# An adaLN block on one core: the second token pair's transposes and splits move up to two steps ahead, the down weights' combinations one step, the odd tile's weights to the end, and one more side of weights is stored

## The chip, the cores and the metric

One Trainium2 chip, of which the kernel uses one core. The metric is device time in microseconds (us), from the first to the last instruction of the launch with what lies around it; lower is better. The kernel before took 540.21 us, the median of 3 runs (540.07 to 543.42).

## What is computed

One transformer block over S = 2048 tokens with D = 512 channels, all in float32:

```python
sa, ca, ga, sb, cb, gb = (silu(c) @ w_mod) cut in six rows of D
h = layernorm(x) * (1 + ca) + sa
x = x + ga * linear_attention(h, wqkv, wo)        # 32 heads of 16, phi(t) = elu(t) + 1 + 1e-6
h = layernorm(x) * (1 + cb) + sb
x = x + gb * (((h @ w_gate) * (h @ w_up)) @ w_down)   # F = 1376 hidden columns
```

The change lies in the last line, the gated feed-forward part.

## The kernel before, in words

**Numbers.** Every float32 operand of a matmul is cut into a high part (a copy in the type fp32r, on ACT) and a low part (value minus high part, on DVE or POOL); the text calls the two together a split. A product is three matmuls: high by high, high by low, low by high. The helper `split` (L202 the high part, L203 the low) does this for activations; `Right.high` (L1105, L1108) and `Right.lows` (L1112) do it for gate and up weights, `w_split` (L1319, L1320) for down weights.

**Tokens.** There are four chunks of 512 tokens. The first pair is chunks 0 and 1, the second pair chunks 2 and 3. The attention part runs up to about 260 us and is not touched.

**Gate and up in steps.** The hidden columns are cut in 11 tiles of 128 (the last, tile 10, has 96). For a pair of chunks and one tile, gate and up are one 2 by 2 block product: the rows are the two chunks, the inner blocks are the two halves of D, the columns are gate and up. It is done with seven block products in place of eight (Strassen's scheme in Winograd's form). The left side has the seven operands a11, a12, a22, s1 to s4 (sums of the pair's blocks, made once for a pair, `Left`); the right side has b11, b21, b22, t1 to t4 (differences of the weights, made for each tile, `Right`: `sums` on L1094, on POOL). One such product is a **step** of seven **points**, in this order: p1 (a11 b11), p5 (s1 t1), p6 (s2 t2), p2 (a12 b21), p7 (s3 t3), p3 (s4 b22), p4 (a22 t4). Each point is six matmuls of 128x512 on TensorE (L1150). There are 19 steps: 0 to 7 are tiles 0 to 7 of the first pair (`FIRST`), 8 to 18 are all tiles of the second pair in the order 7, 10, 8, 9, 0, 1, ... 6 (`LATE`). Even steps use one set of four PSUM banks (named bank in the rows), odd steps from 3 on another (named acc).

Within a step ACT copies one bank to the next, since a later point adds onto it (L1155): after p1 bank a to bank b, which p6 adds to; after p6 bank b to bank c, which p7 adds to. So p7 cannot start before the second of these copies has ended. ACT also copies two banks to SBUF (the tiles u), DVE adds them back (L1212 after p7, L1216 after p3) and multiplies gate with up (L1178, one after p3, one after p4). For tile 10 alone the two products are split at p1 of the next step (`flush`, L202 and L203 on the tiles kh and kl); for the others this is done after all steps.

**Order by hand.** No scheduler moves instructions: each engine runs what the code issues in the order in which it is issued, and waits in that order. A table `plan` gives for (step, point) the extra work that is issued at the end of that point. Each engine has one queue; SP's holds all loads and stores.

**The second pair's left side** (the table at L1886). The normalised chunks 2 and 3 are written to DRAM block by block (`stow`, L1009), read back (`unstow`, L116, tiles u) and turned in blocks by DVE (`flip`, L344, into the tile `wide`); ACT takes each of the four rows of a chunk out of `wide` with scale and shift (`flipped`, L349, tiles f); the sums follow on DVE (L1059, tiles s), then the seven splits (L202, L203, tiles h). `x_park` (L332) writes the residual rows of a chunk of the first pair to DRAM.

**Right sides.** At p7 of step m SP gets the loads of step m+2's weights (four of 128 KB, L1088) and ACT and DVE or POOL split those of step m+1; at p4 POOL makes the differences for m+2. For the steps in `ON_VECTOR` the low parts go to DVE, else to POOL. The sides that the last four steps need (tiles 3 to 6) are stored in DRAM at p1 of steps 3 to 6 (`park`, seven stores of 256 KB, L1127) and fetched one step ahead (`Fetched`, seven loads, L1139).

**Down weights** (`Down.planned`). The down product is a second such scheme over pairs of tiles (8,9), (0,1), (2,3), (4,5), (7,6), which also needs t1 to t4 of the weights: two loads, a scale by gb (L1327), four differences (L1341), seven splits (L1319, L1320), seven stores (L1350). Pair i starts at step 8+2i. The odd tile 10 is loaded at step 8, split at step 9, and combined at p5 of step 11 (`odd_turn`: a difference on DVE, L1399, and a split). After step 18 come the down products (L1412, L1433) up to the end.

**Buffers.** All these tiles share 94 buffers of 256 KB in SBUF; a new tile waits until the last reader of the buffer's tile before it is done, which can be a store.

Of the kernel before, what the change touches and what calls it, by code (L numbers as in the profile page):

```python
# [11 lines left out]
ALU = mybir.AluOpType  # L12
# [12 lines left out]
def tile_adaln_block(  # L25
# [985 lines left out]
    def unstow(ch):  # L1011
        for j in range(NJ):
            blocks[ch, j] = load(stowed[ch, j], "u")
# [251 lines left out]
    def x_park(c):  # L1265
        x_parked[c] = [lift_out(f"x_{c}_{j}", xts[c][j]) for j in range(NJ)]
# [30 lines left out]
    class Down:  # L1297
# [99 lines left out]
        def odd_turn(self):  # L1397
            x = self.odd
            nc.vector.tensor_tensor(x[:, :HALF], x[:, :HALF], x[:, HALF:], op=ALU.subtract)  # L1399
# [41 lines left out]
        def planned(self):  # L1441

            def put(b, point, *does):
                plan.setdefault((self.m + b, point), []).extend(does)

            for n, c in enumerate(self.cs):
                for j in range(NJ):
                    put(2 * n + j // 2 - 3, "p2", lambda c=c, j=j: self.x_store(c, j))
            def odd_load():
                f0, n = fts[ODD]  # L1450
                self.odd = load(w_down[f0:f0 + n, :], "raw")

            put(0, "p2", odd_load)
            put(1, "p6", lambda: nc.vector.tensor_tensor(self.odd, self.odd, gb[:self.odd.shape[0]], op=ALU.mult))
            put(1, "p4", *(lambda n=n: self.w_split(("odd", n), self.odd[:, n * HALF:(n + 1) * HALF]) for n in range(2)))
            put(3, "p5", self.odd_turn)
            for i in range(self.NI):
                a, b = 2 * i, 2 * i + 1
                put(a - 1, "p4", lambda i=i: self.w_load(i))
                put(a, "p1", lambda i=i: self.w_scale(i))  # L1460
                put(a, "p7", lambda i=i: self.w_sum(i, "t1", "t3", "t2", "t4"))
                put(a, "p3", lambda i=i: self.w_parts(i, "b11", "b21"))
                put(a, "p4", lambda i=i: self.w_parts(i, "b22", "t1"))
                put(b, "p2", lambda i=i: self.w_park(i, "b11", "b21"))
                put(b, "p6", lambda i=i: self.w_parts(i, "t2", "t3", low=nc.gpsimd if i > 2 else None))
                put(b, "p3", lambda i=i: self.w_park(i, "b22", "t1"))
                put(b, "p7", lambda i=i: self.w_parts(i, "t4", low=nc.gpsimd if i > 2 else None))
                put(b + 1, "p6", lambda i=i: self.w_park(i, "t2", "t3", "t4"))
                if i + 1 < self.NI:
                    put(b + 3, "p5", lambda i=i: self.h_sum("s1", i))  # L1470
                    put(b + 3, "p6", lambda i=i: self.h_sum("s3", i))

        def planned_first(self):

            def put(b, point, *does):
                plan.setdefault((self.m + b, point), []).extend(does)
# [8 lines left out]
            put(last, "p4", lambda: self.h_split("a12", 0, 1, low=nc.gpsimd))  # L1485

        def x_store(self, c, j):
            if c not in self.x_rows:
# [395 lines left out]
    sums = lambda k, n: lambda: second[k].sum(n)  # L1884
    split_in = lambda k, n: lambda: second[k].into(second_side).split(n)
    for at, does in {  # L1886
        (1, "p4"): [lambda: stow(3, 3)], (2, "p5"): [flips(2, 0)], (2, "p4"): [flips(2, 1)],
        (3, "p1"): [flips(2, 2)], (3, "p5"): [flips(2, 3)], (3, "p6"): [turned(0, 2, "a11")],
        (3, "p3"): [turned(0, 2, "a12")], (3, "p4"): [turned(1, 2, "a11"), lambda: unstow(3)],
        (4, "p1"): [turned(1, 2, "a12")], (4, "p5"): [flips(3, 0)], (4, "p6"): [split_in(0, "a11"), flips(3, 1)],  # L1890
        (4, "p3"): [split_in(0, "a12")], (4, "p4"): [flips(3, 2), split_in(1, "a11")],
        (5, "p1"): [flips(3, 3)], (5, "p6"): [turned(0, 3, "a21")], (5, "p3"): [turned(0, 3, "a22")],
        (5, "p4"): [split_in(1, "a12"), sums(0, "s1"), turned(1, 3, "a21")],
        (6, "p1"): [sums(0, "s3"), turned(1, 3, "a22")], (6, "p5"): [sums(0, "s2")],
        (6, "p6"): [split_in(0, "s1"), split_in(0, "s3")], (6, "p3"): [split_in(0, "s2")], (6, "p4"): [sums(0, "s4"), sums(1, "s1"), sums(1, "s3")],
        (7, "p1"): [sums(1, "s2"), split_in(1, "s1")], (7, "p5"): [sums(1, "s4"), split_in(0, "s4")],
        (7, "p3"): [split_in(1, "s2"), split_in(1, "s3")], (7, "p4"): [split_in(0, "a22")],
        (8, "p1"): [split_in(1, "s4")], (8, "p5"): [split_in(1, "a22")]}.items():
        plan.setdefault(at, []).extend(does)
    free[0] = True  # L1900
    for _ in work:
# [29 lines left out]
```

## Time and profile before

| | |
|---|---|
| median of 3 runs | 540.21 us |
| the profiled execution's own time | 540.03 us |
| its span, first to last instruction | 538.3 us |
| TensorE busy | 528.9 us (98%), 2551 matmuls |
| DVE, ACT, POOL busy | 424.9, 318.2, 157.5 us |
| mean granted TensorE clock | 0.997 |
| DRAM read, written | 66.98 MB, 36.44 MB |

How to read the rows in the prediction. In the timeline a row is: start in us, duration in us, engine, line, operation, output<-input, the partitions and elements, how many instructions were merged; in brackets how long the engine was idle just before and what released it. Matmuls overlap, so a merged row of PE reaches a little into the next one; the starts are what counts. SPq is SP's queue handing out a transfer, not the transfer. In the chain of work that ended last a row is start, duration, engine, tile, line. In the table by stretches the columns are the stretch, its length, busy time and count of each engine asked for, the granted TensorE clock, the busy share of the 16 DMA engines and GB/s.

### The profile page before, as it was taken

The numbers are of one execution on the slowest core, as the hardware profiler recorded it, in microseconds if no ns is written. First come the engines' busy times: TensorE is split into PE (matmuls) and PEld (weight loads), VectorE is DVE, ScalarE is ACT, GpSimd is POOL, SyncE is SP. The second block draws the span as 40 slices with busy tenths as digits, with TensorE's granted clock in tenths as the row PEclk, the third lists the DMA queues.
The fourth block names the chain that finished last, engine by engine and source line by source line (L and its number), as shares of the span: only waits on it lengthen the run. The fifth ranks groups of instructions, "written<-read, shape, count | busy, mean of one in ns | idle before, by whom it ended". The sixth has DMA issues, their size and how long they took to land.

```text
span 538.3 us, 8125 instructions
## 1 busy us (share of the span) xinstructions
PE 528.9 (98%) x2551; PEld 441.8 (82%) x2551; DVE 424.9 (79%) x739; ACT 318.2 (59%) x600; POOL 157.5 (29%) x158
## 2 busy tenths in 40 slices
PE   8999999999999999999999999998999999999997
PEld 6888888888778878878888887786888889998887
DVE  7997879999989888789445699897886657788594
ACT  3696878768678765576566765653634344425530
POOL 2001010000022220085683672797731164100000
PEclk9999999999999999999999999998999999999999
DMA  8902426320166165856079984347199789869776
GB/s 283 387 33 94 141 102 212 92 65 2 41 199 202 34 217 165 285 152 174 28 222 289 367 285 133 114 141 251 61 360 344 245 323 332 279 228 291 224 178 152
DMA packets 99419, 103.97 MB, mean 193 GB/s; under 512 B 25968, under 2 KB 59760, under 8 KB 99376
## 3 DMA queue, kind: packets, MB, share of 16 engines
q1 hardware_dynamic: 95024, 102.41, 58.8%
q10 hardware_dynamic: 4352, 1.05, 0.9%
q8 instruction: 20, 0.33, 0.3%
q14 instruction: 23, 0.19, 0.1%
HBM read 66.98 MB, written 36.44 MB: 192 GB/s over the span
## 4 chain that ended last, share of the span: by engine, by line
PE 94%; DVE 3%; ACT 1%; issue 1%; DMA 0%; DVEq 0%; ACTq 0%
PE bank L1150 18%; PE acc L1150 13%; PE acc L882 8%; PE acc L1412 6%; PE bank L215 4%; PE bank L217 4%; PE bank L216 4%; PE acc L1433 4%; PE bank L1433 4%; PE bank L1412 3%; PE acc L424 3%; PE acc L422 3%; PE acc L423 3%; PE bank L965 2%; PE bank L967 2%; PE bank L966 2%
## 5 line engine op out<-in xcount | busy, mean ns | idle before, releaser
L1150 PE MATMUL bank<-h,w 128*128 128x512 f32 x462 | 106.7, 390 | 0.5 <-ACT bank L1155 0.5
L1150 PEld LDWEIGHTS bank<-h,w 128*128 128x128 f32 x462 | 86.7, 188 | 19.0 <-ACT bank L1155 1.0
L1150 PE MATMUL acc<-h,w 128*128 128x512 f32 (+1 forms) x336 | 79.7, 396 | 3.6 <-ACT acc L1155 3.6
L1150 PEld LDWEIGHTS acc<-h,w 128*128 128x128 f32 (+1 forms) x336 | 62.9, 188 | 19.0 <-ACT acc L1155 4.4
L271 POOL TENSOR_TENSOR rstd<-ve,half 128x2 f32<-128x2 f32 (+3 forms) x13 | 11.8, 910 | 108.3 <-DVE ve L270 65.3
L215 PE MATMUL bank<-w,h 128*128 128x512 f32 x104 | 40.7, 391 | 0.0
L217 PE MATMUL bank<-w,h 128*128 128x512 f32 x104 | 40.6, 391 | 0.0
L216 PE MATMUL bank<-w,h 128*128 128x512 f32 x104 | 40.6, 390 | 0.0
L882 PE MATMUL acc<-w,xh 128*128 128x512 f32 x120 | 37.3, 392 | 0.0
L1155 ACT ACTIVATE bank<-bank 128x512 f32<-128x512 f32 x24 | 14.0, 583 | 38.6 <-PE bank L1150 34.0
L1112 POOL TENSOR_TENSOR w<-raw,w 128x256 fp32r<-128x256 f32 (+3 forms) x24 | 26.6, 1108 | 29.8 <-ACT w L1105 29.8
L1112 POOL TENSOR_TENSOR w<-t,w 128x512 fp32r<-128x512 f32 (+1 forms) x24 | 32.5, 1356 | 0.0
L1412 PE MATMUL acc<-w,kh 128*128 128x256 f32 (+1 forms) x176 | 31.9, 283 | 0.0
L1155 ACT ACTIVATE acc<-acc 128x512 f32<-128x512 f32 (+1 forms) x18 | 10.5, 581 | 35.8 <-PE acc L1150 24.4
L1212 DVE TENSOR_TENSOR u<-bank,u 128x512 f32<-128x512 f32 x11 | 7.6, 687 | 25.6 <-PE bank L1150 20.3
L1412 PEld LDWEIGHTS acc<-w,kh 128*128 128x128 f32 (+1 forms) x176 | 27.6, 192 | 0.2
L882 PEld LDWEIGHTS acc<-w,xh 128*128 128x128 f32 x120 | 22.4, 188 | 5.0 <-DVE w L793 0.3
L422 PE MATMUL acc<-kh,xh 128*128 128x512 f32 x64 | 25.1, 393 | 0.0
L424 PE MATMUL acc<-kl,xh 128*128 128x512 f32 x64 | 25.0, 391 | 0.0
L203 POOL TENSOR_TENSOR w<-raw,w 128x512 fp32r<-128x512 f32 (+1 forms) x7 | 9.9, 1425 | 51.6 <-ACT w L202 46.5
L423 PE MATMUL acc<-kh,xl 128*128 128x512 f32 x64 | 25.0, 390 | 0.0
L1412 PE MATMUL acc<-w,kl 128*128 128x256 f32 x88 | 24.9, 283 | 0.0
(270 smaller groups left out, 1389.9 us busy)
## 6 DMA issues: line engine op xcount, KB each, us to landing
w<-down_t SPq DMA_DIRECT2D x36, 256.0 KB, 5.2
right<-w SPq DMA_DIRECT2D x28, 256.0 KB, 3.7
w<-right SPq DMA_DIRECT2D x28, 256.0 KB, 5.1
w<-down_b SPq DMA_DIRECT2D x27, 256.0 KB, 4.3
raw<-in_w_mod_dram SPq DMA_DIRECT2D x24, 256.0 KB, 4.0
down_t<-w SPq DMA_DIRECT2D x20, 256.0 KB, 5.1
x<-in_A_x_dram SPq DMA_DIRECT2D x16, 256.0 KB, 5.4
x<-x SPq DMA_DIRECT2D x16, 256.0 KB, 3.9
```

What stands on the lines that cost most here:

```text
L215: nc.tensor.matmul(ps, ah, bh, start=i == 0, stop=False)
L216: nc.tensor.matmul(ps, ah, bl, start=False, stop=False)
L217: nc.tensor.matmul(ps, al, bh, start=False, stop=i == n - 1)
L422: nc.tensor.matmul(tacc[k], xh[:, a:b], kh, start=first, stop=False)
L423: nc.tensor.matmul(tacc[k], xl[:, a:b], kh, start=False, stop=False)
L424: nc.tensor.matmul(tacc[k], xh[:, a:b], kl, start=False, stop=last)
L882: nc.tensor.matmul(yps[i], x, y, start=False, stop=k == KD - 1 and x is al, skip_group_check=True)
L1112: sub = lambda out, x, y: (on or nc.gpsimd).tensor_tensor(out, x, f32(y), op=ALU.subtract)
L1150: mm = lambda x, y, **kw: nc.tensor.matmul(ps, x[:, k], y, skip_group_check=True, **kw)
L1155: nc.scalar.activation(out, x, AF.Copy)
L1412: nc.tensor.matmul(ps, x[:, a:b], y, start=start, stop=False, skip_group_check=True)
L1433: nc.tensor.matmul(ps, of[:, x], y, start=start, stop=False, skip_group_check=True)
```

## The change

It changes only the order in which work is issued, and for one tile whether its right side is made twice or stored and fetched.

- Left side of the second pair: the flips move from steps 2 to 5 into steps 2 and 3, the rows from steps 3 to 6 into 2 to 4, the sums from 5 to 7 into 4 to 6, the splits from 4 to 8 into 3 to 7. The read of chunk 3 (`unstow(3)`) moves from p4 of step 3 to p6 of step 2.
- `x_park` of chunks 0 and 1 moves from ahead of step 2 to p3 of steps 5 and 6.
- Down weights: pair i starts at step 7+2i, one step earlier; the odd tile is loaded at step 16, scaled and split at 17, combined at 18, its last low part on DVE and not POOL.
- `AGAIN` is one less: tile 2's side is stored at step 2 and fetched at step 13, and its loads, differences and splits for step 14 fall away.
- `ON_VECTOR` is (2, 4) and not (4, 6).
- At the end, four splits of a11 of the first down product, which stood together at p5 of step 18, are spread over p2 and p3 of step 17 and p1 and p2 of step 18.

```diff
-    AGAIN = len(steps) - 4
+    AGAIN = len(steps) - 5
...
-    ON_VECTOR = (4, 6)
+    ON_VECTOR = (2, 4)
...
         def odd_turn(self):
             x = self.odd
             nc.vector.tensor_tensor(x[:, :HALF], x[:, :HALF], x[:, HALF:], op=ALU.subtract)
-            self.w_split(("odd", "turn"), x[:, :HALF], nc.gpsimd)
+
+        def odd_split(self):
+            self.w_split(("odd", "turn"), self.odd[:, :HALF])
...
-            put(0, "p2", odd_load)
...
-            put(3, "p5", self.odd_turn)
+            put(8, "p2", odd_load)
...
+            put(10, "p2", self.odd_turn)
+            put(10, "p3", self.odd_split)
             for i in range(self.NI):
-                a, b = 2 * i, 2 * i + 1
+                a, b = 2 * i - 1, 2 * i
                 put(a - 1, "p4", lambda i=i: self.w_load(i))
...
-                    put(b + 3, "p5", lambda i=i: self.h_sum("s1", i))
+                    put(b + 4, "p5", lambda i=i: self.h_sum("s1", i))
...
-            put(last, "p5", lambda: self.h_split("a11", *range(self.NI), low=nc.gpsimd))
+            for i, at in enumerate(((last - 1, "p2"), (last - 1, "p3"), (last, "p1"), (last, "p2"))):
+                put(*at, lambda i=i: self.h_split("a11", i, low=nc.gpsimd))
...
-    x_park(0)
-    x_park(1)
...
-        (1, "p4"): [lambda: stow(3, 3)], (2, "p5"): [flips(2, 0)], (2, "p4"): [flips(2, 1)],
...
+        (1, "p4"): [lambda: stow(3, 3)], (2, "p1"): [flips(2, 0)], (2, "p5"): [flips(2, 1)],
+        (2, "p6"): [flips(2, 2), lambda: unstow(3)], (2, "p2"): [flips(2, 3)], (2, "p7"): [turned(0, 2, "a11")],
...
+        (4, "p1"): [turned(0, 3, "a21"), split_in(0, "a12")], (4, "p6"): [turned(0, 3, "a22")],
...
```

**Place 1, ACT in step 4.** The rows run from the copy after p1 (bank_2882) to the one after p6 (bank_2883<-bank_2882), for which p7 waits. Before:

```order
L1155 ACTIVATE bank_2882<-bank_2881 128x512
L349 ACTIVATE f_3362<-wide,col_1355,col_1410 128x512
L1155 ACTIVATE u_3370<-bank_2884 128x512
L1155 ACTIVATE bank_2883<-bank_2882 128x512
L1155 ACTIVATE u_3380<-bank_2882 128x512
```

Now:

```order
L1155 ACTIVATE bank_2882<-bank_2881 128x512
L349 ACTIVATE f_3370<-wide,col_1355,col_1410 128x512
L202 ACTIVATE h_3372<-f_3229 128x512
L1155 ACTIVATE u_3382<-bank_2884 128x512
L1155 ACTIVATE bank_2883<-bank_2882 128x512
L1155 ACTIVATE u_3391<-bank_2882 128x512
```

The row taken out of `wide` was chunk 2's last (f_3362) and is now chunk 3's first (f_3370), which needs all four flips of chunk 3; a split stands behind it, ahead of the copy.

**The same place on DVE**, from the add after step 3's p7 (L1212) on; L1112 are the low parts of step 4's weights. Before:

```order
L1216 TENSOR_TENSOR u_3270<-acc_3150,u_3270 128x512
L1178 TENSOR_TENSOR u_3270<-acc_3147,u_3270 128x512
L1178 TENSOR_TENSOR u_3260<-acc_3149,u_3260 128x512
L344 STREAM_TRANSPOSE wide<-u_3333 128x512
L203 TENSOR_TENSOR h_3383<-f_3272,h_3382 128x512
```

Now:

```order
L1112 TENSOR_TENSOR w_3320<-t_3239,w_3313 128x512
L1216 TENSOR_TENSOR u_3284<-acc_3134,u_3284 128x512
L1178 TENSOR_TENSOR u_3284<-acc_3131,u_3284 128x512
L344 STREAM_TRANSPOSE wide<-u_3180 128x512
L1178 TENSOR_TENSOR u_3275<-acc_3133,u_3275 128x512
L344 STREAM_TRANSPOSE wide<-u_3182 128x512
L203 TENSOR_TENSOR h_3346<-f_3219,h_3345 128x512
```

The first flip of chunk 3 (u_3333) stood here; now the last two do (u_3180, u_3182), behind the low part of step 4's t3 and t4, which stood there before as well.

**Place 2, DVE from p7 of step 9 to p6 of step 10.** u_3886 and u_3895 before, u_3921 and u_3930 now, are tile 10's gate by up products, 96 wide. Before:

```order
L1212 TENSOR_TENSOR u_3886<-acc_3149,u_3886 96x512
L1320 TENSOR_TENSOR w_3942<-t_3835,w_3942 128x256
L1216 TENSOR_TENSOR u_3895<-acc_3150,u_3895 96x512
L1178 TENSOR_TENSOR u_3895<-acc_3147,u_3895 96x512
L1178 TENSOR_TENSOR u_3886<-acc_3149,u_3886 96x512
```

Now:

```order
L1212 TENSOR_TENSOR u_3921<-acc_3133,u_3921 96x512
L1341 TENSOR_TENSOR t_3972<-raw_3902 128x256
L1341 TENSOR_TENSOR t_3973<-raw_3904,raw_3902 128x256
L1341 TENSOR_TENSOR t_3972<-raw_3904,t_3972 128x256
L1341 TENSOR_TENSOR t_3973<-raw_3904,t_3972 128x256
L1216 TENSOR_TENSOR u_3930<-acc_3134,u_3930 96x512
L1178 TENSOR_TENSOR u_3930<-acc_3131,u_3930 96x512
L1320 TENSOR_TENSOR w_3986<-raw_3902,w_3986 128x256
L1320 TENSOR_TENSOR w_3989<-raw_3904,w_3989 128x256
L1178 TENSOR_TENSOR u_3921<-acc_3133,u_3921 96x512
```

The four differences of the next pair of down weights and two low parts now stand ahead of the last product; they stood in step 10 before.

**The same place on ACT**, from the copy after step 10's p1 on. Before:

```order
L1155 ACTIVATE bank_2882<-bank_2881 128x512
L202 ACTIVATE kh_3987<-u_3895 96x512
L202 ACTIVATE kh_3991<-u_3886 96x512
L1155 ACTIVATE u_4003<-bank_2884 128x512
L1155 ACTIVATE bank_2883<-bank_2882 128x512
```

Now:

```order
L1155 ACTIVATE bank_2882<-bank_2881 128x512
L202 ACTIVATE kh_4018<-u_3930 96x512
L202 ACTIVATE kh_4022<-u_3921 96x512
L1155 ACTIVATE u_4032<-bank_2884 128x512
L1155 ACTIVATE bank_2883<-bank_2882 128x512
```

ACT's order is the same; kh_4022 takes the last of the DVE products above, and the copy for p7 stands two rows behind it.

**Place 3, ACT in step 11.** Before, w_4109 is the odd tile's combination:

```order
L1155 ACTIVATE acc_3148<-acc_3147 128x512
L1155 ACTIVATE u_4106<-acc_3150 128x512
L1319 ACTIVATE w_4109<-raw_3804 96x256
L1155 ACTIVATE acc_3149<-acc_3148 128x512
L1155 ACTIVATE u_4119<-acc_3148 128x512
```

Now:

```order
L1155 ACTIVATE acc_3132<-acc_3131 128x512
L1155 ACTIVATE u_4134<-acc_3134 128x512
L1155 ACTIVATE acc_3133<-acc_3132 128x512
L1155 ACTIVATE u_4143<-acc_3132 128x512
```

The split ahead of the copy is gone from this step; it now stands behind p3 of step 18.

More of the change, by code (lines that the diff above doesn't have):

```diff
@@ L1892, in tile_adaln_block @@
[L1892 to L1896, printed above, removed]
@@ new lines, in tile_adaln_block @@
+        (3, "p3"): [flips(3, 2)], (3, "p4"): [flips(3, 3), split_in(0, "a11")],
+        (4, "p1"): [turned(0, 3, "a21"), split_in(0, "a12")], (4, "p6"): [turned(0, 3, "a22")],
+        (4, "p2"): [turned(1, 3, "a21"), split_in(1, "a11")], (4, "p3"): [turned(1, 3, "a22")],
+        (4, "p4"): [sums(0, "s1"), sums(0, "s3"), split_in(1, "a12")],
+        (5, "p1"): [sums(1, "s1"), sums(1, "s3")], (5, "p6"): [split_in(0, "s1")],
+        (5, "p2"): [sums(0, "s2"), split_in(0, "s3")], (5, "p3"): [sums(1, "s2"), split_in(1, "s1"), lambda: x_park(0)],
@@ L1899, in tile_adaln_block @@
+        (5, "p4"): [sums(0, "s4"), split_in(0, "s2")],
+        (6, "p1"): [sums(1, "s4"), split_in(1, "s3")], (6, "p6"): [split_in(1, "s2")],
+        (6, "p2"): [split_in(0, "s4")], (6, "p3"): [split_in(1, "s4"), lambda: x_park(1)],
+        (6, "p4"): [split_in(0, "a22")], (7, "p6"): [split_in(1, "a22")]}.items():
         plan.setdefault(at, []).extend(does)
```

17 lines of the change are left out of this document (7 added, 10 removed).

## The prediction

> **What bounds the kernel now.** The table of engines comes first: TensorE (PE) is busy for 528.9 of the span's 538.3 us, so only its pauses can be won. The waits of PE name one kind of partner, ACT's copy between banks (L1155). PE's timeline then shows where.
>
> ```profile
> 281.96 9.68 PE L1150 MATMUL acc<-h,w 128*128 128x512 f32 x42
> 291.48 8.78 PE L1150 MATMUL bank<-h,w 128*128 128x512 f32 x38
> ...
> 320.04 5.60 PE L1150 MATMUL acc<-h,w 128*128 128x512 f32 x24
> 326.51 4.42 PE L1150 MATMUL acc<-h,w 128*128 128x512 f32 x18 [0.86 <-ACT acc L1155]
> 330.76 9.69 PE L1150 MATMUL bank<-h,w 128*128 128x512 f32 x42
> 340.28 9.83 PE L1150 MATMUL acc<-h,w 128*96 128x512 f32 x42
> 349.95 9.71 PE L1150 MATMUL bank<-h,w 128*128 128x512 f32 x42
> 359.50 5.60 PE L1150 MATMUL acc<-h,w 128*128 128x512 f32 x24
> 367.79 5.84 PE L1150 MATMUL acc<-h,w 128*128 128x512 f32 x18 [2.69 <-ACT acc L1155]
> 373.47 9.68 PE L1150 MATMUL bank<-h,w 128*128 128x512 f32 x42
> ...
> 430.59 5.60 PE L1150 MATMUL bank<-h,w 128*128 128x512 f32 x24
> 436.72 4.38 PE L1150 MATMUL bank<-h,w 128*128 128x512 f32 x18 [0.53 <-ACT bank L1155]
> 440.93 0.40 PE L1412 MATMUL acc<-w,kh 128*128 128x256 f32 x2
> ```
>
> A step without a pause takes 9.52 us (281.96 to 291.48), a matmul 0.227. Three steps are cut after 24 matmuls, that is before p7, which is due 5.44 us after its step's start: step 7 (320.04 to 330.76, 10.72 us), 11 (359.50 to 373.47, 13.97) and 18 (430.59 to 440.93, 10.34). They cost 1.20, 4.45 and 0.82 us over 9.52, 6.47 together. The pauses themselves are 1.03, 2.85 and 0.69 us (326.51 less 325.48, and so on). Step 9, 96 wide, takes 9.67 and stays so.
>
> What ACT did ahead of each late copy stands in its timeline, for step 18 in the chain of work that ended last:
>
> ```profile
> 324.33 0.63 ACT L202 ACTIVATE h<-s 128x512 fp32r<-128x512 f32 x1 [2.09 <-DVE s L1059]
> ...
> 325.87 0.59 ACT L1155 ACTIVATE acc<-acc 128x512 f32<-128x512 f32 x1
> ...
> 366.84 0.42 ACT L1319 ACTIVATE w<-raw 96x256 fp32r<-96x256 f32 x1 [3.76 <-DVE raw L1399]
> 367.17 0.57 ACT L1155 ACTIVATE acc<-acc 128x512 f32<-128x512 f32 x1
> ```
>
> ```profile
> 434.11 2.08 ACT kh L202 x4
> ```
>
> In step 7 a split waited for a sum (L1059) that DVE made late; in step 11 the odd tile's combination waited for DVE (L1399); in step 18 four splits stood in a row. The pause of 2.85 cost 1.60 more than itself, since the granted clock (the column behind PE's count) fell:
>
> ```profile
> 364.95:367.79 2.84, 0.15 (x1) 0.95 0.78 253
> 367.79:373.63 5.84, 5.84 (x19) 0.73 0.93 305
> ```
>
> **What the change removes.** Step 11: the odd tile's split no longer stands before the copy, and nothing else there depends on DVE: 4.45 us. Step 18: ahead of the copy for p7 there is now one split each at p1 and p2 of the scheme's order, the second behind it: 0.82. Step 7: the sums are now issued from p4 of step 4 to p1 of step 6; only one split of a sum still stands ahead of a copy for p7, at p1 of step 6, and its sum is issued at p1 of step 5. DVE may be late with it by a whole step of 9.52 us; that is the cover, and 1.20 the gain. Without the cover it would be a pause like the old one.
>
> Moves that cost nothing by themselves: the side stored and fetched instead of made (seven stores and seven fetches for four loads, four POOL differences and the splits) loads SP and the DMA engines, not PE; its fetch is issued more than a step before step 14 as far as the order of waits tells. The low parts of step 6 go to POOL, which has room between its differences, those of step 2 to DVE, ahead of the add after p3 of step 1. Step 4's low parts stood like that before (the add L1216 at 291.77, quoted below, follows them), and step 4 took its 9.52 whole; that is the cover, and without it the price would be a pause of about the four low parts, 2.5 us.
>
> **What it adds, first place: step 4.** PE's p7 there is due at 291.48 + 5.44 = 296.92. ACT's copy for it now stands behind the first row of chunk 3, which waits for the last flip, which stands on DVE behind the low parts of step 4's weights, which wait for POOL's differences and for the loads. So the loads count.
>
> ```profile
> 269.01 6.70 SPq L1009 DMA_DIRECT2D stowed<-n  x12
> ...
> 280.42 2.27 SPq L1009 DMA_DIRECT2D stowed<-n  x4
> ...
> 284.27 0.47 SPq L1088 DMA_DIRECT2D raw<-in_B_w_up_dram  x1
> 284.83 4.27 SPq L1127 DMA_DIRECT2D right<-w  x7
> 289.85 0.69 SPq L1088 DMA_DIRECT2D raw<-in_B_w_up_dram  x1
> ...
> 291.75 1.87 SPq L116 DMA_DIRECT2D u<-stowed  x4
> ```
>
> ```profile
> 286.78 0.74 POOL L1094 TENSOR_TENSOR t<-raw,t 128x256 f32<-128x256 f32 x1 [0.31 <-DMA raw<-in_B_w_up_dram]
> 288.17 0.74 POOL L1094 TENSOR_TENSOR t<-raw,t 128x256 f32<-128x256 f32 x1
> 293.76 0.74 POOL L1094 TENSOR_TENSOR t<-raw 128x256 f32<-128x256 f32 x1 [4.85 <-DMA raw<-in_B_w_up_dram]
> ```
>
> The twelve stow transfers end at 275.71. Then, without `x_park`, come four stows (2.27), the seven stores of step 2's side (4.27), four reads of `unstow` (1.87): 284.1, and step 4's loads: three of some 0.5 and then the last, at 285.6 (284.27 before). It lands 2.5 us after its start if the queue is light (284.27 to POOL's 286.78), 3.9 if loaded (289.85 to 293.76). POOL's last difference ends 2.13 after that landing (286.78 to 288.91): 290.3 or 291.7. High part 0.63 on ACT and low part 0.69 on DVE with handing over: 291.7 or 293.1.
>
> ```profile
> 291.77 0.69 DVE L1216 TENSOR_TENSOR u<-acc,u 128x512 f32<-128x512 f32 x1
> 292.49 1.29 DVE L1178 TENSOR_TENSOR u<-acc,u 128x512 f32<-128x512 f32 x2
> ...
> 303.52 0.70 DVE L344 STREAM_TRANSPOSE wide<-u 128x512 f32<-128x512 f32 x1
> ```
>
> ```profile
> 293.59 0.81 ACT L349 ACTIVATE f<-wide,col,col 128x512 f32<-128x512 f32 x1
> ```
>
> Then DVE does add, product, flip, product, flip: 0.72 from the add to the next start, 0.6 for each further one (two products take 1.29), 0.70 for the last, 3.2 in all; ACT the row (0.81), a split and a copy (0.51 each: a split, a copy and a split lie between the starts 324.33 and 325.87) and the copy for p7 (0.59), 2.4 in all. It ends at 297.4 or 298.8, PE pauses 0.5 or 1.9 us. A gain is excluded, since step 4 runs at 9.52 now. Nothing quoted tells whether the queue is loaded just then, so I take the middle: 1.2. A pause costs 0.17 more than itself (1.20 against 1.03): **1.37 us**.
>
> **Second place: step 10.** ACT's second split at p1 (tile 10's) now waits for a product that stands behind four differences and two low parts. The trace has the same run of DVE operations in steps 8, 10 and 12, where nothing waited:
>
> ```profile
> 344.12 0.68 DVE L1178 TENSOR_TENSOR u<-bank,u 128x512 f32<-128x512 f32 x1
> ...
> 360.28 2.39 DVE L1341 TENSOR_TENSOR t<-raw,t 128x256 f32<-128x256 f32 x2
> ...
> 365.13 0.68 DVE L1178 TENSOR_TENSOR u<-bank,u 128x512 f32<-128x512 f32 x1
> ...
> 387.76 0.68 DVE L1178 TENSOR_TENSOR u<-bank,u 128x512 f32<-128x512 f32 x1
> ...
> 400.84 0.88 DVE L1341 TENSOR_TENSOR t<-raw,t 128x256 f32<-128x256 f32 x2
> ```
>
> The last product (L1178) ends 14.04, 15.86 and 14.97 us after its step's start (330.76, 349.95, 373.47). The spread is the differences: two take 2.39 us beside POOL's work and 0.88 without. None of the three is more like step 9 by these rows, so I take the middle one, 14.97. Step 9 takes 9.67: the product ends 5.30 into step 10. Split, copy, copy and handing over take 1.73 (0.51 + 0.51 + 0.59 and 0.12), so p7 starts at 7.03, not 5.44: a pause of 1.59, between 0.66 and 2.48; with 0.17, **1.76 us** (0.83 to 2.65).
>
> **Sum.** 540.03 - 6.47 + 1.37 + 1.76 = **536.7 us** on the profiled execution, which lies 0.2 below the median. With both low ends 535.1, with both high ends 538.3.
>
> **Rivals.**
> 1. No new pause: 540.03 - 6.47 = 533.6. For it: DVE was free for 2 us and more at these points in other steps. Against: in both places the order is fixed and the summed rows overrun. Chance 0.12.
> 2. The clock falls after step 10's pause: a pause of 1.03 left it whole, one of 2.85 did not. At the high end, 2.48, it costs the 1.60 of step 11 in place of 0.17: 536.7 + 0.89 + 1.43 = 539.0. Chance 0.15.
> 3. Step 7's pause stays, because the spread-out sums meet POOL's low parts of step 6: 536.7 + 1.20 = 537.9. Chance 0.08.
> 4. Slower than before: SP's queue. From step 2's stores to the first down weights it holds 69 transfers, 16.0 MB (16 of 128 KB, 53 of 256 KB).
>
> ```profile
> 291.64:301.16 9.52, 9.52 (x44) 7.89 (x43) 6.00 (x10) 6.41 (x12) 6.29 (x7) 1.00 1.00 343
> ```
>
> ```profile
> DMA packets 7946, 8.45 MB, mean 264 GB/s; under 512 B 762, under 2 KB 4858, under 8 KB 7943
> ```
>
> At the 343 GB/s of step 4 they take 47 us from 278.0 and land at about 325; at the mean of 264 over 268 to 300 us they take 61, to 339. The down weights are scaled on DVE ahead of step 7's add after p7, and the next copy between banks stands behind their splits. From a landing at about 328.6 each us more is a us of pause, from 332 the kernel is slower than before, at 339 it takes 547. Against it: the mean of 264 holds stretches with nothing queued. Chance 0.04.
>
> By the Trainium skill (TensorE: Matmul & The Clock Gate, section "What's actually happening") the gate closes after an idle window of about 3.4 us. By that neither new pause could close it, and rival 2 would be empty. The trace does not agree as it stands: 2.85 us were enough for a granted clock of 0.73.
>
> **Chances and range.** The forecast has the remaining 0.61. Within 1% is about what a measurement here tells from no change; that is 534.8 to 545.6. Below lies rival 1 and a little of the forecast's low end, 0.13; above, rival 4, 0.04; between, 0.83. The range is 533.8 to 540.0: it takes in both pauses' bounds, rivals 2 and 3 and most of rival 1, and leaves out the slow queue and a clock that falls twice.
>
> **What would show it.** Right: PE's timeline has 9.52 us for steps 7, 11 and 18; a cut after 24 matmuls of step 4, released by ACT L1155, with L349 ahead of it waiting for DVE L344; another in step 10 with L202 waiting for L1178. Step 12 starts about 371, the down products about 438. Wrong: step 4 or 10 whole (rival 1), a granted clock below 1 behind step 10 (2), a split waiting for L1059 in step 7 (3), DVE L1327 waiting for a load in step 7 (4). A pause in the down products, where I expect none, would show that the later odd tile or the fetches collide there.

## The result, and the profile after

| | before | changed |
|---|---|---|
| median of 6 runs each | 540.48 us | 548.27 us |
| ratio, 95% interval | | 1.0139 (1.0116 to 1.0163) |
| span of the profiled execution | 538.3 us | 547.4 us |
| TensorE busy, mean granted clock | 528.9 us, 0.997 | 532.9 us, 0.991 |

The change makes the kernel 1.4% slower, where 536.7 and no measurable change had been forecast. The waits of PE in the profile after (in all, how often, the longest):

```profile
PE bank L1150 <- DVE u L1212: 4.1, 3, 3.0
PE acc L1150 <- DVE u L1212: 2.9, 1, 2.9
...
PE bank L1150 <- ACT bank L1155: 1.7, 1, 1.7
```

In the profile before, L1150 waited for ACT's copy L1155 alone. Now it mostly waits for L1212, DVE's add after p7. PE's timeline shows in which steps:

```profile
282.88 9.68 PE L1150 MATMUL acc<-h,w 128*128 128x512 f32 x42
292.40 5.60 PE L1150 MATMUL bank<-h,w 128*128 128x512 f32 x24
299.73 3.02 PE L1150 MATMUL bank<-h,w 128*128 128x512 f32 x12 [1.73 <-ACT bank L1155]
303.49 1.67 PE L1150 MATMUL bank<-h,w 128*128 128x512 f32 x6 [0.74 <-DVE u L1212]
305.00 8.35 PE L1150 MATMUL acc<-h,w 128*128 128x512 f32 x36
316.25 2.93 PE L1150 MATMUL acc<-h,w 128*128 128x512 f32 x6 [2.91 <-DVE u L1212]
318.98 11.36 PE L1150 MATMUL bank<-h,w 128*128 128x512 f32 x42
330.18 9.68 PE L1150 MATMUL acc<-h,w 128*128 128x512 f32 x42
...
358.89 8.35 PE L1150 MATMUL bank<-h,w 128*128 128x512 f32 x36
367.57 1.65 PE L1150 MATMUL bank<-h,w 128*128 128x512 f32 x6 [0.33 <-DVE u L1212]
369.06 9.70 PE L1150 MATMUL acc<-h,w 128*128 128x512 f32 x42
378.60 8.32 PE L1150 MATMUL bank<-h,w 128*128 128x512 f32 x36
389.95 2.29 PE L1150 MATMUL bank<-h,w 128*128 128x512 f32 x6 [3.03 <-DVE u L1212]
392.03 10.70 PE L1150 MATMUL acc<-h,w 128*128 128x512 f32 x42
...
440.65 9.68 PE L1150 MATMUL bank<-h,w 128*128 128x512 f32 x42
...
450.17 0.40 PE L1414 MATMUL acc<-w,kh 128*128 128x256 f32 x2
```

Steps 7 (330.18), 11 (369.06) and 18 (440.65 to 450.17) are whole, 9.52 or 9.54 us: everything that the change was to remove is gone. But steps 5, 10 and 12 are now cut after 36 matmuls, ahead of p4, and step 4 is cut after 24 and after 36. Steps 6 and 13 have no cut and are longer all the same: the granted clock was 0.84 and 0.90 in them (the rows for both stand in the last section). From start to start, with what each step took before:

| where | before | changed | difference |
|---|---|---|---|
| start of step 0 (nothing changed ahead of it) | 250.68 | 251.19 | +0.51 |
| steps 0 to 2 | 31.28 | 31.69 | +0.41 |
| step 4 | 9.52 | 12.60 | +3.08 |
| step 5 | 9.52 | 13.98 | +4.46 |
| step 6 | 9.52 | 11.20 | +1.68 |
| step 7 | 10.72 | 9.52 | -1.20 |
| step 10 | 9.55 | 10.17 | +0.62 |
| step 11 | 13.97 | 9.54 | -4.43 |
| step 12 | 9.52 | 13.43 | +3.91 |
| step 13 | 9.52 | 10.54 | +1.02 |
| step 18 | 10.34 | 9.52 | -0.82 |

That is +15.69 - 6.45 = +9.24 us, and the spans differ by 9.1. The first row is scatter: step 0 starts between 250.68 and 251.65 us in the profiles of this document, in no order that goes with their times. Some 4.5 us of the sum are the clock and not the waiting itself: p4 of step 5 took 2.73 us and that of step 12 2.08, where p4 of step 4, after a pause as well but at a clock of 1.00, took 1.51; steps 6 and 13 are the rest.

**Why p4 waits for an add.** p4 accumulates onto the bank that p7 has just filled, so DVE must have read that bank (L1212) first. p7 ends 30 x 0.227 = 6.8 us into a step, p4 is due at 8.17, the add takes 0.68: it must start by about 7.5. DVE runs in order, so everything issued to it between p4 of one step and p2 of the next must be done by then. Step 5 on DVE, before:

```profile
308.07 0.69 DVE L1212 TENSOR_TENSOR u<-acc,u 128x512 f32<-128x512 f32 x1 [2.66 <-PE acc L1150]
```

DVE was idle for 2.66 us ahead of this add (in brackets), after two flips and one low part. The same stretch in the changed kernel, whose step 5 starts at 305.00:

```profile
302.14 0.69 DVE L203 TENSOR_TENSOR h<-f,h 128x512 fp32r<-128x512 f32 x1 [2.39 <-ACT h L202]
302.75 0.68 DVE L1212 TENSOR_TENSOR u<-bank,u 128x512 f32<-128x512 f32 x1
...
305.81 2.38 DVE L1059 TENSOR_TENSOR s<-f,f 128x512 f32<-128x512 f32 x2
308.11 1.22 DVE L203 TENSOR_TENSOR h<-f,h 128x512 fp32r<-128x512 f32 x1
309.26 2.37 DVE L1059 TENSOR_TENSOR s<-f,f 128x512 f32<-128x512 f32 x2
...
313.85 1.75 DVE L203 TENSOR_TENSOR h<-s,h 128x512 fp32r<-128x512 f32 x1
315.52 0.68 DVE L1212 TENSOR_TENSOR u<-acc,u 128x512 f32<-128x512 f32 x1
```

Five sums and three low parts (two of the eight are left out in the fence), without a gap, stand ahead of the add, which starts 10.52 us into the step. In step 4 (first two rows) the add at 302.75 stands behind a low part (L203) that waited 2.39 us for its high part on ACT, which stood behind two rows out of `wide`: DVE was idle, and the add was not let past.

### The profile page after: what moved, and what is told of

Same layout as the page of the kernel before. It is cut to its first block, busy times and chain, and to the rows that moved or that the text cites. A ratio compares the mean times of both kernels' runs of the same rounds, so it can differ in the third digit from the quotient of the medians.

```text
span 547.4 us, 8168 instructions
## 1 busy us (share of the span) xinstructions
PE 532.9 (97%) x2551; PEld 443.3 (81%) x2551; DVE 426.5 (78%) x740; ACT 316.9 (58%) x596; POOL 153.2 (28%) x149
## 4 chain that ended last, share of the span: by engine, by line
PE 80%; DVE 7%; DMA 4%; issue 3%; ACT 2%; SPq 1%; POOL 1%; POOLq 0%; DVEq 0%; ACTq 0%
PE bank L1150 15%; PE acc L1150 10%; PE acc L882 7%; PE acc L1414 6%; PE acc L1435 4%; PE bank L1435 4%; PE bank L217 3%; PE bank L215 3%; PE bank L1414 3%; PE bank L216 3%; PE acc L424 2%; PE acc L422 2%; PE acc L423 2%; PE bank L965 2%; PE bank L967 2%
## 5 line engine op out<-in xcount | busy, mean ns | idle before, releaser
L1150 PE MATMUL bank<-h,w 128*128 128x512 f32 x462 | 110.2, 396 | 6.0 <-DVE u L1212 4.1
L1150 PEld LDWEIGHTS bank<-h,w 128*128 128x128 f32 x462 | 87.9, 191 | 26.5 <-DVE u L1212 5.4
L1150 PE MATMUL acc<-h,w 128*128 128x512 f32 (+1 forms) x336 | 80.2, 398 | 2.9 <-DVE u L1212 2.9
L1150 PEld LDWEIGHTS acc<-h,w 128*128 128x128 f32 (+1 forms) x336 | 63.5, 189 | 18.3 <-DVE u L1212 3.3
L1155 ACT ACTIVATE acc<-acc 128x512 f32<-128x512 f32 (+1 forms) x18 | 10.5, 581 | 46.8 <-PE acc L1150 32.0
L1112 POOL TENSOR_TENSOR w<-raw,w 128x256 fp32r<-128x256 f32 (+3 forms) x22 | 26.3, 1196 | 35.7 <-ACT w L1105 35.7
L1155 ACT ACTIVATE bank<-bank 128x512 f32<-128x512 f32 x24 | 14.0, 582 | 35.5 <-PE bank L1150 30.8
L1112 POOL TENSOR_TENSOR w<-t,w 128x512 fp32r<-128x512 f32 (+1 forms) x22 | 31.3, 1421 | 0.0
L203 POOL TENSOR_TENSOR w<-raw,w 128x512 fp32r<-128x512 f32 (+1 forms) x7 | 9.7, 1393 | 51.6 <-ACT w L202 46.5
L1212 DVE TENSOR_TENSOR u<-acc,u 128x512 f32<-128x512 f32 (+1 forms) x8 | 5.5, 689 | 23.7 <-PE acc L1150 19.4
```

What stands on the lines that cost most here:

```text
L1112: sub = lambda out, x, y: (on or nc.gpsimd).tensor_tensor(out, x, f32(y), op=ALU.subtract)
L1150: mm = lambda x, y, **kw: nc.tensor.matmul(ps, x[:, k], y, skip_group_check=True, **kw)
L1155: nc.scalar.activation(out, x, AF.Copy)
```

## The experiments

Two theories. **Theory 1, VectorE's order** (VectorE is DVE in the rows, GpSimd is POOL, ScalarE is ACT): the loss comes from work that now stands ahead of the add L1212 in DVE's queue, stretched where POOL works at the same time. **Theory 2, SP's queue:** the loads of steps 4 and 5 are late, because one more side is stored ahead of them, and the later pauses follow from that. Differences are against the kernel before on the same chip, whose median was 540.6 to 540.9 us in these runs.

### The down weights back at their old steps

```
-                a, b = 2 * i - 1, 2 * i
+                a, b = 2 * i, 2 * i + 1
...
-                    put(b + 4, "p5", lambda i=i: self.h_sum("s1", i))
+                    put(b + 3, "p5", lambda i=i: self.h_sum("s1", i))
```

> The changed kernel with the down weights' combinations at their old steps. Theory 1 (VectorE's order: what is moved ahead of the add L1212 delays p4): steps 10, 12 and 13 lose their 0.65 + 3.91 + 1.02 us, 548.3 - 5.6 = 542.7 us. Theory 2 (SP's queue is late from step 4 on and the later pauses follow from that): steps 12 and 13 still pause, above 546 us.

Measured: 543.37 us, ratio 1.0050 (1.0035 to 1.0065). Steps 10, 12 and 13 are whole, steps 4 and 5 still cost 3.99 and 3.24 us. Theory 1's number is right within 0.7, but in part by luck: against the changed kernel step 4 lost another 0.91 us and step 11 1.48, while steps 5 and 6 took 1.22 and 1.65 less. Step 11, which had been whole, is now cut for the add:

```profile
375.71 1.66 PE L1150 MATMUL acc<-h,w 128*128 128x512 f32 x6 [1.21 <-DVE u L1212]
```

So with the odd tile gone from step 11, the down weights' old place has a pause of 1.2 us there by itself; the run with the odd tile alone shows it too.

### The two sums of the first down pair one step later

```
-                    put(b + 4, "p5", lambda i=i: self.h_sum("s1", i))
+                    put(b + 4 + (i == 0), "p5", lambda i=i: self.h_sum("s1", i))
...
```

> The changed kernel with the two sums L1374 of the first down pair moved from step 12 to step 13. Theory 1: 1.76 us leave VectorE's queue ahead of step 12's add L1212, the pause of 3.03 falls to about 1.3 and the clock holds, steps 12 and 13 cost 1.5 instead of 4.9: 544.9 us. If the order on VectorE is not what matters, nothing changes: 548.3 us.

Measured: 542.84 us, 1.0033 (1.0019 to 1.0046): 5.4 us better than the changed kernel, where 3.4 were expected. Step 12 is whole (377.83 to 387.35). The changed kernel ahead of step 12's add, and then this run:

```profile
384.64 0.68 DVE L1374 TENSOR_TENSOR s<-u,u 128x512 f32<-128x512 f32 x1
...
386.40 2.89 DVE L1320 TENSOR_TENSOR w<-t,w 128x256 fp32r<-128x256 f32 x2
```

```profile
383.53 1.08 DVE L1320 TENSOR_TENSOR w<-t,w 128x256 fp32r<-128x256 f32 x3
```

Without the two L1374, three L1320 take 1.08 us; behind them (the first row is the first of the two) two took 2.89. They now run ahead of POOL's large low parts (from 385.18 in this run, from 385.89 in the changed kernel) and not beside them. An operation taken out of the queue so gave more than its own time. By its size the sum was wrong, by its kind theory 1 holds.

### Without POOL's large low parts in steps 5 and 6

```
-                l = self.tile("w", F32R)
-                sub(l, x, h)
+                l = h if skip else self.tile("w", F32R)
+                if not skip:
+                    sub(l, x, h)
...
+            rights[n].lows(nc.vector if n in ON_VECTOR else on, n in (5, 6))
```

> The changed kernel, leaving out the three large low parts of the weights of steps 5 and 6 that GpSimd makes (the high part stands in their place); VectorE's and ScalarE's orders are unchanged. Theory 1 with GpSimd's work stretching VectorE's: the sums and low parts in step 5 take 0.7 and not 1.2 us, the add L1212 is about 3 us earlier, step 5's pause falls from 2.91 to below 0.5 and step 6's clock comes back: about 542.6 us. If it is the number of operations in VectorE's queue alone: 548.3 us, with the pauses as they are.

The kernel leaves out three low parts in each of the two steps, with the high parts in their place, so it no longer computes the block. Measured: 544.16 us, 1.0062 (1.0042 to 1.0082), 4.1 better than the changed kernel. The groups of DVE in step 5 (busy time, mean ns of one), in the changed kernel and in this run, whose lines from there on count one more:

```profile
L1059 DVE TENSOR_TENSOR s<-f,f 128x512 f32<-128x512 f32 x4 | 4.8, 1228 | 0.0
...
L1212 DVE TENSOR_TENSOR u<-acc,u 128x512 f32<-128x512 f32 x1 | 0.7, 678 | 0.0
```

```profile
L1059 DVE TENSOR_TENSOR s<-f,f 128x512 f32<-128x512 f32 x4 | 3.0, 783 | 0.0
...
L1213 DVE TENSOR_TENSOR u<-acc,u 128x512 f32<-128x512 f32 x1 | 0.7, 676 | 0.0
```

A sum falls from 1228 to 783 ns, the pause of step 5 from 2.91 to 0.69, and step 6 is whole. DVE's orders are the same in both, so the number of its operations alone is not the cause: POOL's work at the same time stretches those that read two tiles in SBUF, and not the add, which reads one bank of PSUM. In the changed kernel the add (315.52 to 316.20) ran beside this POOL row:

```profile
315.01 1.72 POOL L1112 TENSOR_TENSOR w<-raw,w 128x512 fp32r<-128x512 f32 x1
```

The Trainium skill (SBUF — State Buffer, section "Who interferes with whom") says this of a VectorE instruction with two SBUF inputs beside a GpSimd one that reads SBUF; the trace agrees, 678 and 676 ns for the add, 1228 against 783 for the sum.

### The low parts of steps 4 and 6, and not 2 and 4, on VectorE

```
-    ON_VECTOR = (2, 4)
+    ON_VECTOR = (4, 6)
```

> The changed kernel with the low parts of steps 4 and 6, not of 2 and 4, on VectorE. They stand behind the add L1212 of step 5, and GpSimd has no low parts in the second half of step 5. Stretching by GpSimd: the operations from 311 us on take half, the pause of step 5 is 1 to 1.5 us shorter, about 546 us. Number of operations alone: VectorE has four more, 548.3 us or above.

Measured: 548.63 us, 1.0120 (1.0065 to 1.0175). The time is what the second expectation gave, but the first one's reason shows as well: step 5's pause fell by 2 us (1 to 1.5 were expected), and as much came up in step 6. The four executions lay between 544.99 and 551.17 us; the trace is of one at 550.97.

```profile
315.58 1.65 PE L1150 MATMUL acc<-h,w 128*128 128x512 f32 x6 [0.93 <-DVE u L1212]
...
327.76 2.51 PE L1150 MATMUL bank<-h,w 128*128 128x512 f32 x6 [2.37 <-DVE u L1212]
```

Four low parts behind step 5's add push sums and splits of steps 5 and 6 against the next add. Steps 0 to 2 took 31.28 us here, as before the change: the 0.41 there belongs to the low parts of step 2 on VectorE.

### Without the one more stored side

```
-    AGAIN = len(steps) - 5
+    AGAIN = len(steps) - 4
```

> The changed kernel without the one more stored side (tile 2's weights are made twice as before). Theory 1: step 4's loads start earlier and its 3.08 us shrink, steps 5 and 6 stay as they are: 545.2 to 548.3 us. Theory 2: steps 4 to 6 are clean, 548.3 - 9.2 = 539.1 us.

Measured: 547.67 us, 1.0123 (1.0108 to 1.0138). Steps 4 to 6 still cost 2.73, 4.09 and 0.75 us over 9.52, and the time is only 0.6 us below the changed kernel's. So theory 2 is not what slows the changed kernel: POOL's last difference for step 4 ends at 287.70 here and at 292.81 there, and yet ACT's row (L349) starts hardly earlier in its step, 4.63 against 4.97 us:

```profile
286.96 0.74 POOL L1094 TENSOR_TENSOR t<-raw,t 128x256 f32<-128x256 f32 x1
```

```profile
291.63 1.18 POOL L1094 TENSOR_TENSOR t<-raw,t 128x256 f32<-128x256 f32 x1
```

```profile
296.49 0.82 ACT L349 ACTIVATE f<-wide,col,col 128x512 f32<-128x512 f32 x1 [2.49 <-DVE wide L344]
```

```profile
297.37 0.81 ACT L349 ACTIVATE f<-wide,col,col 128x512 f32<-128x512 f32 x1 [2.83 <-DVE wide L344]
```

These are, two by two, POOL's last difference and ACT's row, each here and in the changed kernel; step 4 starts at 291.86 us here and at 292.40 there. But for 0.34 us it is DVE's low parts, products and flips that set the row, not the loads.

### The old table for the left side, with the stored side

```
-    ON_VECTOR = (2, 4)
+    ON_VECTOR = (4, 6)
...
+    x_park(0)
+    x_park(1)
...
-        (1, "p4"): [lambda: stow(3, 3)], (2, "p1"): [flips(2, 0)], (2, "p5"): [flips(2, 1)],
+        (1, "p4"): [lambda: stow(3, 3)], (2, "p5"): [flips(2, 0)], (2, "p4"): [flips(2, 1)],
...
```

> The changed kernel with the old table of the second pair's left side, x_park and the choice of steps whose low parts VectorE makes; the stored side of tile 2 stays. Theory 1: steps 4, 5 and 6 lose their 3.08 + 4.46 + 1.68 and step 3's 0.4, step 7's 1.20 comes back: 548.3 - 8.4 = 539.9 us. Theory 2: the seven stores are still ahead of step 4's loads, so step 4 still pauses by 2 to 3 us and step 5 with it: 543 to 547 us.

Measured: 547.48 us, 1.0122 (1.0106 to 1.0137). Here theory 1 missed by 7.6 us: step 5 is whole, but step 4 took 13.24 us, as theory 2 said, and steps 6 and 7 took 0.73 and 1.08 us more than in the kernel before. Three more runs were made to part the two.

### The odd tile and the end alone, then with the stored side, then with x_park moved

The first is the kernel before with

```
-            put(0, "p2", odd_load)
+            put(8, "p2", odd_load)
...
-            put(3, "p5", self.odd_turn)
+            put(10, "p2", self.odd_turn)
+            put(10, "p3", self.odd_split)
...
-            put(last, "p5", lambda: self.h_split("a11", *range(self.NI), low=nc.gpsimd))
+            for i, at in enumerate(((last - 1, "p2"), (last - 1, "p3"), (last, "p1"), (last, "p2"))):
...
```

the second has `AGAIN = len(steps) - 5` besides, the third also `x_park` at p3 of steps 5 and 6 and not ahead of step 2.

> The kernel before with only the odd tile's move to the end and the spread of the four splits in step 18. Both theories touch nothing but steps 11 and 18 here: 540.5 - 4.45 - 0.82 = 535.2 us. If the odd tile at the end costs something there (a pause in steps 16 to 18 or in the down products), it stays above 536.

> The run with the odd tile alone (536.8 us), and one change more: tile 2's side is stored and fetched. In the run with the old table step 4 took 13.24 and not 9.52 us. If the stored side did that by itself (SP's queue), step 4 takes about 13 us here too: 540.5 us or more. If it only did so together with the earlier down weights or the stored side is harmless: 536.8 us.

> The run with the stored side alone (541.0 us), and x_park moved to p3 of steps 5 and 6 as in the changed kernel. If the eight transfers of x_park ahead of the seven stores are what makes step 4's loads late, its loads start some 4.6 us earlier, step 4 is whole again and the time falls to that without the stored side, 536.8 to 537.5 us. If the stores alone do it: 541 us.

Measured: 536.82 us, 0.9927 (0.9912 to 0.9942); 541.03, 1.0003 (0.9980 to 1.0026); 536.42, 0.9919 (0.9902 to 0.9935). SP's queue in the second and the third run:

```profile
276.57 4.59 SPq L332 DMA_DIRECT2D x<-x  x8
...
283.60 3.85 SPq L1127 DMA_DIRECT2D right<-w  x7
287.55 0.59 SPq L1088 DMA_DIRECT2D raw<-in_B_w_gate_dram  x1
```

```profile
278.27 3.85 SPq L1127 DMA_DIRECT2D right<-w  x7
282.23 0.59 SPq L1088 DMA_DIRECT2D raw<-in_B_w_gate_dram  x1
```

Step 4's first load starts at 287.55 behind `x_park` and the stores, at 282.23 behind the stores alone. In the second run PE waits in step 4 for the weights themselves:

```profile
294.20 0.73 PE L1150 MATMUL bank<-h,w 128*128 128x512 f32 x2 [0.30 <-ACT w L1108]
```

So theory 2 names a real cost, 4.2 us, but one of which the changed kernel pays 0.6 at most, since it moves `x_park` too. The first run missed its 535.2 by 1.6, and that is step 11: it took 11.03 us and not 9.52, with a wait of 1.21 us for the add L1212 ahead of p4, since the old pause ahead of p7 had covered a late add behind it. (Steps 6 and 7 took 10.24 and 10.01 where they took 9.52 and 10.72 before; the two cancel, and why they differ is not shown.)

### And two splits of step 7 behind the copy

```
-        (7, "p1"): [sums(1, "s2"), split_in(1, "s1")], (7, "p5"): [sums(1, "s4"), split_in(0, "s4")],
+        (7, "p1"): [sums(1, "s2")], (7, "p5"): [sums(1, "s4")], (7, "p6"): [split_in(1, "s1"), split_in(0, "s4")],
```

> As the run with the odd tile alone, and in step 7 the two splits ahead of the copy for p7 moved behind it. If the pause of step 7 is nothing but ACT's order, another 1.20 goes: 534.0 us. If VectorE is what is late there, the pause moves to a later point of step 7 or to step 8 and the time stays at 535.2.

Measured: 537.04 us, 0.9936 (0.9919 to 0.9952), no gain over 536.82. Step 7's pause went from the copy (p7) to the add (p4, 0.79 us): VectorE was late there, as the second expectation had it.

### Only step 4 mended

```
-        (4, "p1"): [turned(0, 3, "a21"), split_in(0, "a12")], (4, "p6"): [turned(0, 3, "a22")],
-        (4, "p2"): [turned(1, 3, "a21"), split_in(1, "a11")], (4, "p3"): [turned(1, 3, "a22")],
+        (4, "p1"): [split_in(0, "a12")], (4, "p6"): [turned(0, 3, "a21")],
+        (4, "p7"): [split_in(1, "a11"), turned(0, 3, "a22")], (4, "p3"): [turned(1, 3, "a21"), turned(1, 3, "a22")],
```

> The changed kernel with only step 4 mended: the first row of chunk 3 behind the copy for p7, one row and one split behind the add L1212. If the two pauses of step 4 come from these orders alone, step 4 takes 9.52 and not 12.60 us, and steps 5, 6, 10 and 12 stay: 548.3 - 3.1 = 545.2 us. If the lateness is only handed on, step 5's pause grows and the time stays near 548 us.

Measured: 546.62 us, 1.0110 (1.0095 to 1.0125). Step 4 is whole, but the time is only 1.65 us better than the changed kernel's, about half of step 4's 3.08:

```profile
315.11 2.83 PE L1150 MATMUL acc<-h,w 128*128 128x512 f32 x6 [4.75 <-DVE u L1212]
```

Step 5 starts earlier and its pause grows from 2.91 to 4.75: DVE's run of sums is what ends late there, whenever PE gets to it.

### All of it behind the add

In steps 4 to 7 rows, sums and splits are issued behind L1212 of their step, and from step 8 on the low parts of t2 and t3 and the sums L1374 as well; the steps are those of the changed kernel, or one later for some sums and splits. The second run has the old number of stored sides besides.

```
-        (5, "p1"): [sums(1, "s1"), sums(1, "s3")], (5, "p6"): [split_in(0, "s1")],
-        (5, "p2"): [sums(0, "s2"), split_in(0, "s3")], (5, "p3"): [sums(1, "s2"), split_in(1, "s1"), lambda: x_park(0)],
-        (5, "p4"): [sums(0, "s4"), split_in(0, "s2")],
+        (5, "p7"): [sums(0, "s1"), sums(0, "s3"), sums(1, "s1"), split_in(0, "s1")],
+        (5, "p3"): [sums(1, "s3"), sums(0, "s2"), split_in(0, "s3"), lambda: x_park(0)],
+        (5, "p4"): [sums(1, "s2"), split_in(1, "s1")],
...
-                put(b, "p6", lambda i=i: self.w_parts(i, "t2", "t3", low=nc.gpsimd if i > 2 else None))
+                put(b, "p7", lambda i=i: self.w_parts(i, "t2", "t3", low=nc.gpsimd if i > 2 else None))
...
```

> The changed kernel with nothing put into another step except where the points force it: in steps 4 to 7 the rows, sums and splits are issued behind the add L1212 of their step (p7, p3, p4) and not ahead of it, and in the steps from 8 on the low parts of t2 and t3 and the sums L1374 too. Theory 1, that only what stands ahead of the add counts: the pauses of steps 4, 5, 6, 10 and 12 go, of 548.3 us some 15 go: 533.5 to 535 us. If VectorE simply has too much work there in all, the pauses come back one step later: 540 us or more.

> The run with the work behind the add, and without the one more stored side. If the stored side costs something by SP's queue (the seven stores ahead of step 4's loads), this is faster than the run with it by that, 1 us or more; by theory 1 with the queue on time both are equal within 0.5 us, 533.5 to 535 us.

Measured: 537.25 us, 0.9921 (0.9890 to 0.9951), and 537.87, 0.9932 (0.9909 to 0.9955). The same work in another order, a few sums and splits of it one step later, is 11 us faster than the changed kernel. Steps 4, 5, 10, 12 and 13 are whole. What is missed to 535 is step 6, 12.28 us (311.17 to 323.45):

```profile
314.85 5.74 PE L1150 MATMUL bank<-h,w 128*128 128x512 f32 x24 [0.80 <-ACT bank L1155]
321.96 1.66 PE L1150 MATMUL bank<-h,w 128*128 128x512 f32 x6 [1.37 <-DVE u L1212]
```

There the second expectation is right in part: step 5's sums run over into step 6, which loses 2.76 us. A gain from leaving the stored side out does not show: the two intervals overlap.

### The best of both

The run with the odd tile alone, with the work of steps 6 and 7 and the low parts of t2 and t3 behind the add.

```
-                put(b, "p6", lambda i=i: self.w_parts(i, "t2", "t3", low=nc.gpsimd if i > 2 else None))
+                put(b, "p7", lambda i=i: self.w_parts(i, "t2", "t3", low=nc.gpsimd if i > 2 else None))
...
-        (6, "p1"): [sums(0, "s3"), turned(1, 3, "a22")], (6, "p5"): [sums(0, "s2")],
-        (6, "p6"): [split_in(0, "s1"), split_in(0, "s3")], (6, "p3"): [split_in(0, "s2")],
-        (7, "p1"): [sums(1, "s2"), split_in(1, "s1")], (7, "p5"): [sums(1, "s4"), split_in(0, "s4")],
-        (7, "p3"): [split_in(1, "s2"), split_in(1, "s3")],
+        (6, "p1"): [sums(0, "s3"), turned(1, 3, "a22")],
+        (6, "p7"): [sums(0, "s2"), split_in(0, "s1"), split_in(0, "s3")], (6, "p3"): [split_in(0, "s2")],
+        (7, "p7"): [sums(1, "s2"), split_in(1, "s1"), split_in(0, "s4")],
+        (7, "p3"): [sums(1, "s4"), split_in(1, "s2"), split_in(1, "s3")],
```

> The kernel before with the odd tile at the end, and with the sums, splits and low parts that stand ahead of the add L1212 in steps 6, 7 and 11 put behind it. Theory 1: the pauses left in the run with the odd tile alone, 0.43 + 0.19 and some VectorE lateness in step 7 and 1.21 in step 11, go: 536.8 - 1.8 = 535.0 us. If VectorE's total work is the limit, they reappear in steps 8 and 12: 536.8 us.

Measured: 535.20 us, 0.9874 (0.9831 to 0.9918), faster than both kernels. Steps 4 to 10 and 18 are whole; two waits for the add, 0.55 us each in steps 11 and 13, are all that is left.

## Why the prediction was wrong

| term | forecast | measured |
|---|---|---|
| pauses of steps 7, 11 and 18 go | -6.47 | -6.45 |
| step 4 | +1.37 | +3.08 |
| step 10 | +1.76 | +0.62 |
| low parts of step 2 on DVE | 0 | +0.41 |
| sums and splits one or two steps earlier (steps 5, 6) | 0 | +4.46, +1.68 |
| down weights one step earlier (steps 12, 13) | 0 | +3.91, +1.02 |
| before step 0 | 0 | +0.51 |

**What the change removes** was right to 0.02 us in sum. For step 11 there was luck: "nothing else there depends on DVE" was wrong, since its add was late as well, by 1.2 us. That showed only when the odd tile left and the down weights stayed; here the down weights moved away with it.

**The step that failed** is the sentence on the moved sums: "DVE may be late with it by a whole step of 9.52 us; that is the cover". It looked only at who waits for the sums' results. What stands behind them on DVE's queue was not named, and that is the add that frees p4's bank, with idle time of 2.66 us ahead of it in step 5 before. Five sums and three low parts were put there, in the place of two flips and one low part. At 0.68 us each they are 5.4 us; beside POOL's work they took 9.7 (305.81 to 315.52). The run without POOL's low parts gives 3.47 of step 5's 4.46 and all of step 6's 1.68 back, the run with the work behind the add all of step 5's, though step 6 then loses 2.76. The sum also gave each new pause only 0.17 us beyond its length, where the fallen clock took some 4.5 us in this trace.

**The same omission** was made with the down weights: they were costed in step 10 alone, not in step 12, where L1320 and L1374 now meet ahead of the add. Step 12's add had 1.77 us of idle time ahead of it before, behind the same two L1374 and the scaling:

```profile
380.54 0.69 DVE L1212 TENSOR_TENSOR u<-bank,u 128x512 f32<-128x512 f32 x1 [1.77 <-PE bank L1150]
```

**Step 4:** the pause ahead of p7 came as described, ACT's row waiting for DVE's flip, at the upper bound: 299.73 against 292.40 + 5.44 = 297.84, 1.89 us. The reason was wrong: "So the loads count" does not hold but for 0.34 us, as the run without the stored side shows. A second pause, 1.04 ahead of p4 (303.49 against 299.73 + 12 x 0.227 = 302.45), was not foreseen. Nor does the loss simply add to the others: mended alone, step 4 gives 1.65 us.

**Step 10** was overrated: the pause ahead of p7 did not come, since the last product ended 3.22 us into the step and not 5.30; the wait there was for the add.

```profile
361.43 0.68 DVE L1178 TENSOR_TENSOR u<-acc,u 96x512 f32<-96x512 f32 x1
```

**The rivals.** Rival 4 gave 547 us, near the result, but for another reason: no scale of the down weights waited in step 7, and step 7 is whole. That no new pause comes (1) fell with step 4; the clock did fall (2), but behind steps 5 and 12, not 10; step 7's pause (3) went. None of them had the add.

**The low parts of step 2** were put at nothing, since step 4's had cost nothing before. That did not hold whole: they cost 0.41 us.

## What to carry to other kernels

Before moving work on an in-order engine, list that engine's instructions with a deadline (here one add per step, due 7.5 us into it) and the idle time ahead of each, and charge every moved instruction to the first deadline behind it, not only to its own reader. Price it at what it takes beside the other engines that run then: here VectorE's operations with both inputs in SBUF took 1.23 us in the mean beside GpSimd's work, in place of 0.68. A wait that is removed may have covered a smaller one in the same step, so look up what was waiting behind it before counting the whole of it as gain.

## What was not expected of the hardware

The granted clock did not follow from the length of a pause. With the old places for the down weights step 5 paused as long as in the changed kernel, and in the profiled execution the clock stayed whole (columns as in the prediction: stretch, busy time and count of PE, PEld, DVE, ACT and POOL, clock, DMA share, GB/s). The changed kernel first, from p4 of step 5 and of step 12 each to the end of the next step, then that run, from p4 of step 5:

```profile
316.25:318.98 2.73, 2.73 (x7) 2.15 (x7) 2.69 (x4) 0.20 (x2) 2.73 (x3) 0.50 1.05 402
318.98:330.18 11.20, 11.20 (x44) 9.06 (x42) 7.78 (x11) 7.18 (x14) 6.26 (x7) 0.84 0.58 210
389.95:392.03 2.08, 2.08 (x6) 1.66 (x7) 2.04 (x3) 0.00 (x0) 0.47 (x1) 0.69 1.00 338
392.03:402.57 10.54, 10.54 (x44) 8.60 (x43) 4.31 (x9) 3.66 (x8) 0.00 (x0) 0.90 0.84 313
```

```profile
316.86:318.37 1.51, 1.51 (x6) 1.24 (x7) 1.48 (x3) 0.04 (x2) 1.51 (x2) 1.00 1.05 400
318.37:327.92 9.55, 9.55 (x44) 7.88 (x42) 8.97 (x12) 7.37 (x14) 7.53 (x8) 1.00 0.87 329
```

2.91 us of idle time left a clock of 0.50 and then 0.84 in one, 2.90 us left 1.00 in the other; 4.75 us in the run with step 4 mended cost 2.62 us for the six matmuls of p4 in place of 1.51, about as much as 2.91 did (2.73), and less in the step behind it (9.98 us, against 11.20). Nor does one trace stand for its kernel in this: the four executions of the run with the old places had mean granted clocks of 1.000, 0.994, 0.996 and 0.996, and the profiled one is the first. In the ten of the run with the two sums later the mean clock lay between 0.991 and 1.000, and the time between 545.21 and 541.31 us, longest where the clock was lowest. So a step's length in one trace holds a part, here up to 1.7 us, that the next execution may not have. The prediction had taken the pause's length as the measure. What decides stays open.
